# Attention and a mixture of experts in one kernel: another order of the last batch's units, of its routing products and of expert 0's evictions

## The chip, the cores and the metric

The kernel runs on one core of one Trainium2 chip. The metric is the device time of one execution in microseconds. Before the change it was 704.88 us, the median of three runs (702.8, 704.88 and 707.19).

## What is computed

Eight batches of 576 tokens pass through attention with eight heads of 64; heads 0 to 3 see a local window of 32 keys, heads 4 to 7 the keys at the same place modulo 32. Its output (4608 rows of 512) goes through a mixture of 16 experts in 4 groups:

```python
scores = np.where(masks[None], scale * q @ k.transpose(0, 1, 3, 2), -1e9)
attn   = softmax(scores) @ v                      # (8, 8, 576, 64), then x = rows of 512
g_idx  = argmax(x @ w_group)                      # one of 4 groups
e_idx  = argmax(xg @ w_expert[g])                 # one of 4 experts in it
ye     = relu(xg @ w1[g, e]) @ w2[g, e]           # 512 -> 1024 -> 512
out[token] = g_w * e_w * ye                       # weights: the two softmax values
```

## The kernel before

**Attention.** A batch is ten units. Unit j = 2u is strided unit u (heads 4 to 7), unit j = 2u + 1 is local unit u (heads 0 to 3). A unit has four parts: the score products (L206 strided, L244 local), the softmax on VectorE and ScalarE (L183 to L188; L253 to L259), the transposes of the probabilities (L212, L265) with ScalarE's copy of them out of PSUM (L215, L268), and the products with v (L222, L276) with VectorE's scaling into `xs` or `xl` (L194, L195). `attention_step` issues the scores of unit s, the transposes of unit s-4 and, at odd s, the products with v of units s-7 and s-6. In the text S0 to S4 are the strided and L0 to L4 the local units of the last batch, in the order S0 L0 S1 L1 S2 L2 S3 L3 S4 L4.

**Routing.** `logits_steps` transposes a batch's output (`loc` L328, `strd` L347) and copies it out of PSUM (L319, in the last batch L316); each of its pieces is called by `after(j)` some steps after the output of unit j. Seven batches make their logits with split float products (L361, L363). The last makes them with 24 float products of 20 columns (`rows`, L381), four for each of six tiles of 96 tokens: two of the chunks `early` (the strided heads) and two of `late` (the local heads). Then `choose` (VectorE, L415 to L423), `ranks` (TensorE, L432 to L437), `slots` and `onehots` (L459 to L487) and `table` (L491, L869) turn logits into the slots of every expert. The last batch's chain depends on itself alone, but for two sums over the batches: `k.run`, and the table of batch 6.

**Experts.** `slot_tokens` (L501) gives the indices, GpSimd gathers expert 0's rows in three blocks of 128 (L587), TensorE transposes them (L599, four for each block, one into each of PSUM banks 0 to 3), ScalarE and VectorE evict them as a high and a low half (L606, L607), and the products of the 16 experts follow (L626, L679). The first half of expert 0's first weights is loaded and split while the last batch runs (`first_half`: L569 loads, L576 ScalarE, L577 VectorE and GpSimd).

**Dummy products.** `k.spin` issues products of 512 columns (L844) that nobody reads, in places where TensorE would stand still.

**What sets the order.** Each engine works off its own queue in order. In the attention TensorE's order is the order of the code; from the last loop on, and on the other engines throughout, a planner sets it from the dependences and its own costs. The semaphores that it sets guard a PSUM bank as a whole.

Of the kernel before, what the change touches and what calls it, by code (L numbers as in the profile page):

```python
# [9 lines left out]
F32 = mybir.dt.float32  # L10
# [295 lines left out]
def logits_steps(tc, k, b, xs, xl, v):  # L306
# [16 lines left out]
    def loc(u0):  # L323
        pt = k.ps_t.next()
        w = 128 if u0 < 4 else 64
        for j, u in enumerate((u0, u0 + 1) if u0 < 4 else (4,)):
            for c in range(2):
                i = nc.tensor.transpose(pt[:, c * 256 + j * 128:c * 256 + j * 128 + w],  # L328
                                    xl[0:w, u * 256 + c * 128:u * 256 + (c + 1) * 128],
                                    k.ident[0:w, 0:w])  # L330
        if u0 == 4:
            k.spin(b, 1, i, 5)
        n = 256 if u0 < 4 else 64
        evac(lambda x: x[:, 0:2, u0 * 128:u0 * 128 + n],
             pt.rearrange("p (c x) -> p c x", c=2)[:, :, 0:n],
             lambda t: t[:, :2 * n].rearrange("p (c x) -> p c x", c=2))
# [50 lines left out]
    if last:  # L387
        lg = k.bank[1][0:TB, 0:NTB * 20].rearrange("p (t e) -> p t e", e=20)
        k.split_x, k.row = [], None
        steps = [(0, lambda: rows(range(NTB - 1), late)), (1, lambda: rows(range(NTB), early)),  # L390
                 (2, lambda: (rows(range(NTB - 1, NTB), late), k.spin(b, 2, k.row)))]
    else:
        steps = [(4, lambda: mm(0, early + late)), (5, lambda: mm(1, early + late)), (7, back)]
    return lg, {3: lambda: loc(0), 7: lambda: loc(2), 9: lambda: loc(4), 2: lambda: strd(0),
                6: lambda: strd(2), 8: lambda: strd(4)}, steps


def routing_steps(tc, k, b, lg, v, xd):
# [28 lines left out]
    def ranks():  # L427
        wide = lambda x, m: x.broadcast_to([TB, m, 16])
        with ExitStack() as order:
            if b == B - 2:  # L430
                order.enter_context(tc.issue_after(k.row.ins))
            nc.tensor.matmul(pr, k.tri, o16.rearrange("p t e -> p (t e)"), start=True, stop=True)  # L432
# [7 lines left out]
        k.spin(b, 10, i)  # L440
# [22 lines left out]
    t = (3, 5) if b == B - 1 else (7, 11) if b == B - 2 else (7, 10)  # L463
# [67 lines left out]
class Moe:  # L531
# [62 lines left out]
    def xpose(self, xs, first=False):  # L594

        nc, k = self.nc, self.k
        for blk in range(NB):
            for c in range(4):
                self.tp = nc.tensor.transpose(  # L599
                    self.bank(c)[:, blk * 128:(blk + 1) * 128].bitcast(F32R),  # L600
                    xs[blk][:, c * 128:(c + 1) * 128].bitcast(F32R), k.identr)
            if first:
                k.spin(B - 1, 6 if blk == NB - 1 else 3, self.tp, 6)
        for c in range(4):
            pt = self.bank(c)
            last = (nc.scalar.copy(self.xH[:, c, :], pt[:, :CAP]),  # L606
                    nc.vector.tensor_tensor(self.xL[:, c, :], pt[:, :CAP],  # L607
                                            self.xH[:, c, :].bitcast(F32), op=ALU.subtract))
        return last
# [190 lines left out]
def build_all(nc, d, out):  # L800
    k = Ctx()
    with tile.TileContext(nc, schedule_with_timeline_sim=True) as tc, ExitStack() as top:
# [33 lines left out]
        k.pTs = Ring([lp.tile([128, 512], F32, name=f"pTs{i}") for i in range(2)])  # L836
        tasks, now = [], [0]
# [16 lines left out]
        def batch(b, xs, xl):  # L854
# [12 lines left out]
            def table():  # L867
                k.spin(b, 16, st["add"]())
                nc.vector.tensor_tensor(k.tab, k.tab, k.misc[:, 0:2 * NSL], op=ALU.add)  # L869

            def after(j):
                store_x(tc, k, b, xd, xs, xl, j)
                if j in parts:
                    tasks.append((now[0] + (2 + j % 2 if b < B - 1 else 0), parts[j]))
# [12 lines left out]
        with ExitStack() as ms:  # L887
# [18 lines left out]
            for t in k.pT.t + k.pTs.t:  # L906
                nc.gpsimd.memset(t, 1.0)
# [24 lines left out]
            for b in range(B):  # L932
# [51 lines left out]
                for j, u in enumerate(us):  # L984
# [5 lines left out]
            k.ps_t = Ring([k.ps_t.next(), k.ps_t.next()] + k.bank[0:3])  # L990
# [58 lines left out]
```

## Time and profile before

| | us |
|---|---|
| median of 3 runs | 704.88 |
| the profiled execution | 706.36 |
| its span, first to last instruction | 704.6 |
| start to the first score product of the last batch | 173.9 |
| from there to the end of the last product with v | 38.4 (to 212.3) |
| to the end of the last batch's logits | 5.9 (to 218.2) |
| to the first product of expert 0 | 18.6 (to 236.8) |
| the 16 experts to the end of the span | 467.8 |

Times in a trace count from the span's start. A row of the timeline gives start, duration, engine, line, operation, output and input, and the number of instructions merged in it; in brackets stands the idle time ahead of it and what ended that. "PEclk" is the granted clock of TensorE, 1.00 for 2.4 GHz and 0.50 for 1.2 GHz. DVE is VectorE, ACT ScalarE, POOL GpSimd, PE TensorE, PEld its weight loads, SP the queue that issues most DMAs.

### The profile page before, as it was taken

The numbers are of one execution on the slowest core, as the hardware profiler recorded it, in microseconds if no ns is written. First come the engines' busy times: TensorE is split into PE (matmuls) and PEld (weight loads), VectorE is DVE, ScalarE is ACT, GpSimd is POOL, SyncE is SP. The second block draws the span as 40 slices with busy tenths as digits, with TensorE's granted clock in tenths as the row PEclk, the third lists the DMA queues.
The fourth block names the chain that finished last, engine by engine and source line by source line (L and its number), as shares of the span: only waits on it lengthen the run. The fifth ranks groups of instructions, "written<-read, shape, count | busy, mean of one in ns | idle before, by whom it ended". The sixth has DMA issues, their size and how long they took to land. (4 is left out here: it accounts for less than half of the span.)

```text
span 704.6 us, 15310 instructions
## 1 busy us (share of the span) xinstructions
PE 665.9 (95%) x5652; PEld 581.0 (82%) x5653; DVE 440.7 (63%) x1037; ACT 374.8 (53%) x725; POOL 259.3 (37%) x300
## 2 busy tenths in 40 slices
PE   4889999999889999999999999999999999999995
PEld 4778877877776789898898998998988989989893
DVE  8667788778856474566457656767644666545420
ACT  3666667666761473565456445656444564444421
POOL 7054556456642443134233332343240432411111
PEclk9999999999997999999999999999999999999998
DMA  9999899996341775457555474576473564744001
GB/s 274 244 270 251 214 265 246 239 236 172 123 118 33 220 256 184 151 164 252 178 187 193 171 237 136 210 271 198 152 263 124 196 220 135 260 133 149 18 18 38
DMA packets 58232, 130.34 MB, mean 185 GB/s; under 512 B 11672, under 2 KB 22168, under 8 KB 57440
## 3 DMA queue, kind: packets, MB, share of 16 engines
q1 hardware_dynamic: 50432, 109.72, 52.4%
q0 software_dynamic: 7680, 18.91, 7.5%
q8 instruction: 89, 1.46, 0.9%
q14 instruction: 31, 0.25, 0.1%
HBM read 112.86 MB, written 22.04 MB: 191 GB/s over the span
## 5 line engine op out<-in xcount | busy, mean ns | idle before, releaser
L555 DVE TENSOR_TENSOR wL<-raw,wH 128x1024 fp32r<-128x1024 f32 x122 | 145.8, 1235 | 80.9 <-ACT wH L554 75.1
L554 ACT CAST wH<-raw 128x1024 fp32r<-128x1024 f32 x124 | 124.5, 1068 | 74.8 <-PE bank L679 30.1
L626 PE MATMUL bank<-xH,wH 128*128 128x304 f32 (+10 forms) x512 | 152.9, 299 | 0.0
L626 PE MATMUL bank<-xL,wH 128*128 128x304 f32 (+10 forms) x512 | 152.7, 298 | 0.0
L626 PE MATMUL bank<-xH,wL 128*128 128x304 f32 (+10 forms) x512 | 152.7, 298 | 0.0
L663 POOL DMA_INDIRECT out<-y,idx x48 | 51.1, 1065 | 192.0 <-ACT y L657 172.9
L679 PE MATMUL bank<-wH,hH 128*128 128x512 f32 x288 | 113.3, 401 | 1.0 <-DVE hL L645 0.6
L679 PE MATMUL bank<-wL,hH 128*128 128x512 f32 x288 | 114.2, 396 | 0.0
L644 ACT ACTIVATE hH<-bank 128x384 fp32r<-128x384 f32 x128 | 62.9, 497 | 91.9 <-PE bank L626 86.2
L679 PE MATMUL bank<-wH,hL 128*128 128x512 f32 x288 | 111.0, 396 | 0.1
L645 DVE SCALAR_TENSOR_TENSOR hL<-bank,hH 128x384 fp32r<-128x384 f32 x128 | 68.8, 554 | 66.2 <-ACT hH L644 65.6
L626 PEld LDWEIGHTS bank<-xH,wH 128*128 128x128 f32 x512 | 96.5, 188 | 0.8
L626 PEld LDWEIGHTS bank<-xL,wH 128*128 128x128 f32 x512 | 96.5, 189 | 0.7
L626 PEld LDWEIGHTS bank<-xH,wL 128*128 128x128 f32 x512 | 96.5, 188 | 0.0
L587 POOL DMA_INDIRECT xg<-xd,idx x48 | 70.7, 1473 | 19.7 <-issue 10.7
L679 PEld LDWEIGHTS bank<-wH,hH 128*128 128x128 f32 x288 | 54.1, 188 | 14.6 <-issue 1.7
L679 PEld LDWEIGHTS bank<-wH,hL 128*128 128x128 f32 x288 | 54.3, 188 | 13.9 <-issue 0.6
L679 PEld LDWEIGHTS bank<-wL,hH 128*128 128x128 f32 x288 | 54.3, 188 | 12.2
L320 POOL CAST xH_r<-xf 128x512 fp32r<-128x512 f32 (+4 forms) x42 | 30.5, 726 | 75.5 <-ACT xf L319 75.5
L657 ACT ACTIVATE y<-bank,xg 128x512 f32<-128x512 f32 x48 | 31.3, 686 | 41.4 <-PE bank L679 41.4
L649 POOL CAST hP<-hH 128x512 fp32r<-128x512 f32 x16 | 9.8, 613 | 108.7 <-issue 99.1
L206 PE MATMUL bank<-sqk 128*108 128x108 f32 (+1 forms) x320 | 42.7, 279 | 6.9 <-DMA sqk<-sq 3.7
(135 smaller groups left out, 1058.3 us busy)
## 6 DMA issues: line engine op xcount, KB each, us to landing
raw<-w SPq DMA_DIRECT2D x124, 512.0 KB
vl<-vl SPq DMA_DIRECT2D x7, 877.5 KB
vs<-vs SPq DMA_DIRECT2D x7, 650.0 KB
sqk<-sqk SPq DMA_DIRECT2D x14, 324.0 KB
kl<-kl SPq DMA_DIRECT2D x7, 608.0 KB
xd<-xl SPq DMA_DIRECT2D x16, 256.0 KB
ql<-ql SPq DMA_DIRECT2D x7, 576.0 KB
sqk<-sqk SPq DMA_DIRECT2D x14, 252.0 KB
```

What stands on the lines that cost most here:

```text
L206: nc.tensor.matmul(ps[0:n, h * n:(h + 1) * n], t[:, 0:n], t[:, 2 * n:3 * n], start=True, stop=True)
L320: v.tensor_copy(sl(xH), t)
L554: nc.scalar.copy(H[:, d], r)
L555: low[j % len(low)].tensor_tensor(L[:, d], r, H[:, d].bitcast(F32), op=ALU.subtract)
L587: self.nc.gpsimd.indirect_dma_start(out=xg, out_offset=None, in_=self.xd, in_offset=bass.IndirectOffsetOnAxis(ap=self.k.idx[:, c:c + 1], a ...
L626: self.nc.tensor.matmul(ps[:, :N], a[:, c, cols], x[:, c, :N], start=(n == 0), stop=(n == last))
L644: nc.scalar.activation(self.hH[:, f, :], ps, AF.Relu)
L645: nc.vector.scalar_tensor_tensor(self.hL[:, f, :], ps, 0.0, self.hH[:, f, :].bitcast(F32), ALU.max, ALU.subtract)
L649: nc.gpsimd.tensor_copy(self.hP[:, :, i * 64:i * 64 + 64], h[:, :, s].bitcast(F32))
L657: nc.scalar.activation(y, ps, AF.Copy, scale=w)
L663: i = self.sc = nc.gpsimd.indirect_dma_start(out=self.out, out_offset=bass.IndirectOffsetOnAxis(ap=k.idx[:, c:c + 1], axis=0), in_=y, in_o ...
L679: i = nc.tensor.matmul(ps, a[:, f, s], w[:, f, :], start=(n == 0), stop=(n == 23))
```

## The change

The last batch runs its units in the order S0 S1 L0 S2 L1 S3 L2 S4 L3 L4, with two more buffers for transposed probabilities (`pE`). Its transposes go in other pieces, and its logits in four pieces, of tiles 0 to 1, 2 to 3, 0 to 3 and 4 to 5. Around the routing there are 4 dummy products behind the logits for 2, 6 behind the ranks for 10, 14 behind the table for 16, and the one with the last transposes is gone; the 12 between expert 0's transposes stay. Expert 0's three blocks are evicted in two parts, the first two blocks after the second's transposes, and the third after its own. The ranks of batch 6 no longer stand behind the last row of logits.

```diff
-    def loc(u0):
+    def loc(*us):
         pt = k.ps_t.next()
-        w = 128 if u0 < 4 else 64
-        for j, u in enumerate((u0, u0 + 1) if u0 < 4 else (4,)):
+        u0, n = us[0], 0
+        for u in us:
+            w = 128 if u < 4 else 64
...
-        if u0 == 4:
-            k.spin(b, 1, i, 5)
...
-        steps = [(0, lambda: rows(range(NTB - 1), late)), (1, lambda: rows(range(NTB), early)),
-                 (2, lambda: (rows(range(NTB - 1, NTB), late), k.spin(b, 2, k.row)))]
+        steps = [(0, lambda: rows((2, 3), late)), (0, lambda: rows((4, 5), early)),
+                 (0, lambda: (rows((4, 5), late), k.spin(b, 4, k.row)))]
+        return lg, {1: [], 3: [lambda: loc(0, 1)], 2: [lambda: strd(0)], 6: [lambda: strd(2)],
+                    5: [lambda: rows((0, 1), late), lambda: loc(2)], 8: [lambda: strd(4)],
+                    9: [lambda: rows(range(4), early), lambda: loc(3, 4)]}, steps
...
-        with ExitStack() as order:
-            if b == B - 2:
-                order.enter_context(tc.issue_after(k.row.ins))
-            nc.tensor.matmul(pr, k.tri, o16.rearrange("p t e -> p (t e)"), start=True, stop=True)
+        nc.tensor.matmul(pr, k.tri, o16.rearrange("p t e -> p (t e)"), start=True, stop=True)
...
-        k.spin(b, 10, i)
+        k.spin(b, 6, i)
...
-    t = (3, 5) if b == B - 1 else (7, 11) if b == B - 2 else (7, 10)
+    t = (3, 5) if b == B - 1 else (7, 9) if b == B - 2 else (7, 10)
...
-        for c in range(4):
-            pt = self.bank(c)
-            last = (nc.scalar.copy(self.xH[:, c, :], pt[:, :CAP]),
-                    nc.vector.tensor_tensor(self.xL[:, c, :], pt[:, :CAP],
-                                            self.xH[:, c, :].bitcast(F32), op=ALU.subtract))
+            if blk == NB - 1 or first and blk == NB - 2:
+                x = slice(blk * 128 if first and blk == NB - 1 else 0, (blk + 1) * 128)
+                for c in range(4):
+                    pt = self.bank(c)
+                    last = (nc.scalar.copy(self.xH[:, c, x], pt[:, x]),
+                            nc.vector.tensor_tensor(self.xL[:, c, x], pt[:, x],
+                                                    self.xH[:, c, x].bitcast(F32), op=ALU.subtract))
...
-                k.spin(b, 16, st["add"]())
+                k.spin(b, 14, st["add"]())
...
-                if j in parts:
-                    tasks.append((now[0] + (2 + j % 2 if b < B - 1 else 0), parts[j]))
+                for f in parts.get(j, ()):
+                    tasks.append((now[0] + (2 + j % 2 if b < B - 1 else 4 * (j == 2)), f))
...
-                for j, u in enumerate(us):
+                if b == B - 1:
+                    p, q, r = k.pTs.next(), k.pTs.next(), k.pE[0]
+                    k.pTs = Ring([p, q, p, r, q, p, r])
+                    k.pT = Ring([k.pT.next() for _ in range(6)] + k.pE[1:])
+                for j in range(10) if b < B - 1 else (0, 2, 1, 4, 3, 6, 5, 8, 7, 9):
+                    u = us[j]
...
-            k.ps_t = Ring([k.ps_t.next(), k.ps_t.next()] + k.bank[0:3])
+            k.ps_t = Ring([k.ps_t.next(), k.ps_t.next(), k.bank[0], k.bank[2]])
```

The order of the built programs shows where this reaches the other engines' queues. Lines of the changed kernel stand up to eight higher or lower than in the kernel before; PSUM bank n is `bank_(67+n)`.

**Place 1.** ScalarE at the first two pieces of expert 0's weights (`raw`, then `raw_1`), before the change: the copy of batch 6's transposes into `xf` stands between the two casts.

```order
L576 CAST wH_2853<-raw 128x512
L319 COPY xf<-bank_70 128x432
L576 CAST wH_2853<-raw_1_2864 128x512
L484 ACTIVATE rhs_t<-ohh,sm_c 96x6x48
L215 COPY pTs_125<-bank_71 126x504
```

And now:

```order
L575 CAST wH_2857<-raw 128x512
L575 CAST wH_2857<-raw_1_2868 128x512
L319 COPY xf<-bank_70 128x432
L483 ACTIVATE rhs_t<-ohh,sm_c 96x6x48
L268 COPY pT_124<-bank_71 96x512
```

The cast of `raw_1` has moved ahead of the copy out of `bank_70`. On TensorE the next transposes into `bank_70` (four of `xl`) stand behind the scores of L2 and the transposes of L0.

**Place 2.** ScalarE at the copy of batch 6's third strided piece (128x216), before the change:

```order
L259 ACTIVATE pr_120<-pr_120,mx 128x96 x2
L188 ACTIVATE pr_119<-pr_119 108x432
L259 ACTIVATE pr_120<-pr_120,mx 128x96 x2
L215 COPY pTs_126<-bank_71 108x432
L576 CAST wH_2853<-raw 128x512
L319 COPY xf<-bank_70 128x216
```

And now:

```order
L259 ACTIVATE pr_119<-pr_119,mx 128x96
L188 ACTIVATE pr_120<-pr_120 108x432
L268 COPY pT_123<-bank_71 96x512
L575 CAST wH_2857<-raw 128x512
L259 ACTIVATE pr_121<-pr_121,mx 128x96 x4
L319 COPY xf<-bank_70 128x216
```

Both times four exponentials of L3 (L259; `pr_120` before, `pr_121` now) stand ahead of the copy, but now L3's scores come after S4's, and on VectorE L3's maxima stand behind the outputs of S0 and S1 and the split of `raw_3`. TensorE has, ahead of the transposes that wait for this copy, also the four of `strd(0)` of the last batch, which need the output of S1.

**Place 3.** VectorE behind the last batch's logits (`bank_68`), before the change: the addition of batch 6's table (`tab`), for which VectorE waits for TensorE, stands third.

```order
L415 TENSOR_REDUCE mx<-bank_68 96x30
L417 TENSOR_TENSOR dl<-bank_68,mx 96x120
L869 TENSOR_TENSOR tab<-tab,bank_74 128x96
L418 SCALAR_TENSOR_TENSOR val<-dl,sm_c 96x120
L447 TENSOR_REDUCE sm<-ex 96x30
L421 TENSOR_REDUCE vm<-val 96x30
L422 TENSOR_TENSOR oh<-val,vm 96x120
L423 TENSOR_TENSOR o_3444<-oh 96x96
```

And now:

```order
L417 TENSOR_REDUCE mx<-bank_68 96x30
L419 TENSOR_TENSOR dl<-bank_68,mx 96x120
L420 SCALAR_TENSOR_TENSOR val<-dl,sm_c 96x120
L423 TENSOR_REDUCE vm<-val 96x30
L871 TENSOR_TENSOR tab<-tab,bank_74 128x96
L446 TENSOR_REDUCE sm<-ex 96x30
L424 TENSOR_TENSOR oh<-val,vm 96x120
L425 TENSOR_TENSOR o_3476<-oh 96x96
```

The addition has moved two steps back in the chain, behind `val` and `vm`. On TensorE the products that it waits for stand behind the logits in both, with 2 dummies between before and 4 now. At expert 0 the four transposes of the third block now each wait for VectorE as well as (the first) for the gather; before, they waited for the gather alone. On TensorE 20 of the 24 products of the logits stand behind the last product with v, before (6 and 14) as now (9, 4 and 7).

## Rows read from the trace of the kernel before

**Rows 1.** Busy time by stretch: TensorE, weight loads, VectorE, ScalarE, GpSimd; granted clock; DMA.
```profile
187.00:197.00 10.00, 6.55 (x101) 5.77 (x100) 9.88 (x33) 8.24 (x21) 8.62 (x12) 1.00 0.77 220
197.00:212.30 15.30, 14.89 (x194) 11.82 (x194) 7.94 (x28) 8.57 (x20) 5.04 (x7) 0.89 0.34 107
212.30:218.20 5.90, 5.83 (x57) 5.55 (x56) 3.55 (x13) 1.48 (x4) 2.59 (x6) 0.80 0.32 84
218.20:226.20 8.00, 6.49 (x32) 3.15 (x31) 4.89 (x18) 0.84 (x2) 0.94 (x4) 0.51 0.04 0
226.20:236.80 10.60, 8.89 (x45) 4.27 (x43) 3.71 (x15) 1.76 (x5) 7.50 (x7) 0.84 0.44 118
236.80:704.00 467.20, 457.82 (x2710) 410.51 (x2708) 266.88 (x344) 233.16 (x360) 139.51 (x123) 1.00 0.52 175
```

**Rows 2.** Timeline of TensorE in the last batch's attention.
```profile
189.75 0.60 PE L328 MATMUL bank<-ident,xl 128*128 128x128 f32 x4
190.28 0.56 PE L244 MATMUL bank<-kl,ql 64*64 64x96 f32 x16
192.12 0.64 PE L265 MATMUL bank<-ident,pr 128*96 128x128 f32 x4 [1.28 <-ACT pTs L215]
...
197.04 0.33 PE L328 MATMUL bank<-ident,xl 64*128 64x64 f32 x2 [1.42 <-ACT xf L319]
```

**Rows 3.** Timeline of ScalarE in the same stretch.
```profile
190.55 0.62 ACT L576 CAST wH<-raw 128x512 fp32r<-128x512 f32 x1 [1.22 <-DMA raw<-w]
...
191.51 0.56 ACT L215 COPY pTs<-bank 126x504 f32<-126x504 f32 x1
...
196.65 0.34 ACT L319 COPY xf<-bank 128x216 f32<-128x216 f32 x1
```

**Rows 4.** Waits of the queue that issues DMAs, 170 to 200 us.
```profile
SPq L569 <- PE bank L276: 2.1, 1, 2.1
```

**Rows 5.** Timeline of VectorE: two splits of expert 0's weights.
```profile
192.31 0.67 DVE L577 TENSOR_TENSOR wL<-raw,wH 128x512 fp32r<-128x512 f32 x1
...
194.29 1.71 DVE L577 TENSOR_TENSOR wL<-raw,wH 128x512 fp32r<-128x512 f32 x1
```

**Rows 6.** Timeline of TensorE from the last logits to the table.
```profile
212.51 1.20 PE L381 MATMUL bank<-cst,xH_r 128*96 128x20 f32 x12
...
214.69 3.51 PE L381 MATMUL bank<-cst,xH_r 128*96 128x20 f32 x28
...
218.85 0.69 PE L491 MATMUL bank<-rhs_t,ohl 96*128 96x96 bf16 x6
221.05 0.24 PE L432 MATMUL bank<-o,tri 96*96 96x96 bf16 x1 [1.51 <-DVE o L423]
...
221.63 4.43 PE L844 MATMUL bank<-iota 128*128 128x512 bf16 x10
...
225.93 0.48 PE L491 MATMUL bank<-rhs_t,ohl 96*128 96x96 bf16 x6
```

**Rows 7.** Timeline of VectorE in that stretch.
```profile
219.57 0.26 DVE L869 TENSOR_TENSOR tab<-tab,bank 128x96 f32<-128x96 f32 x1 [0.74 <-PE bank L491]
...
223.83 0.45 DVE L482 TENSOR_TENSOR rhs_t<-ohh,blk 96x288 bf16<-96x288 bf16 x1
```

**Rows 8.** Timeline of TensorE at expert 0.
```profile
231.23 0.54 PE L599 MATMUL bank<-identr,xg 128*128 128x128 f32 x4 [1.37 <-DMA xg<-xd,idx]
...
232.78 0.69 PE L599 MATMUL bank<-identr,xg 128*128 128x128 f32 x4 [0.35 <-DMA xg<-xd,idx]
...
234.26 0.99 PE L599 MATMUL bank<-identr,xg 128*128 128x128 f32 x4
235.05 2.11 PE L844 MATMUL bank<-iota 128*128 128x512 bf16 x6
236.81 0.49 PE L626 MATMUL bank<-xH,wH 128*128 128x296 f32 x1
```

**Rows 9.** Timeline of VectorE at expert 0.
```profile
235.56 1.95 DVE L607 TENSOR_TENSOR xL<-bank,xH 128x384 fp32r<-128x384 f32 x4 [6.53 <-ACT xH L606]
```

More of the change, by code (lines that the diff above doesn't have):

```diff
@@ L321, in evac @@
         v.tensor_tensor(sl(xL), t, sl(xH).bitcast(F32), op=ALU.subtract)
-    def loc(u0):
+    def loc(*us):
         pt = k.ps_t.next()
-        w = 128 if u0 < 4 else 64
-        for j, u in enumerate((u0, u0 + 1) if u0 < 4 else (4,)):
+        u0, n = us[0], 0
+        for u in us:
+            w = 128 if u < 4 else 64
             for c in range(2):
-                i = nc.tensor.transpose(pt[:, c * 256 + j * 128:c * 256 + j * 128 + w],
+                nc.tensor.transpose(pt[:, c * 256 + n:c * 256 + n + w],
                                     xl[0:w, u * 256 + c * 128:u * 256 + (c + 1) * 128],
                                     k.ident[0:w, 0:w])
-        if u0 == 4:
-            k.spin(b, 1, i, 5)
-        n = 256 if u0 < 4 else 64
+            n += w
         evac(lambda x: x[:, 0:2, u0 * 128:u0 * 128 + n],
@@ L389, in logits_steps @@
         k.split_x, k.row = [], None
-        steps = [(0, lambda: rows(range(NTB - 1), late)), (1, lambda: rows(range(NTB), early)),
-                 (2, lambda: (rows(range(NTB - 1, NTB), late), k.spin(b, 2, k.row)))]
+        steps = [(0, lambda: rows((2, 3), late)), (0, lambda: rows((4, 5), early)),
[3 more added lines that the diff above has]
+                    9: [lambda: rows(range(4), early), lambda: loc(3, 4)]}, steps
     else:
         steps = [(4, lambda: mm(0, early + late)), (5, lambda: mm(1, early + late)), (7, back)]
-    return lg, {3: lambda: loc(0), 7: lambda: loc(2), 9: lambda: loc(4), 2: lambda: strd(0),
-                6: lambda: strd(2), 8: lambda: strd(4)}, steps
+    return lg, {3: [lambda: loc(0, 1)], 7: [lambda: loc(2, 3)], 9: [lambda: loc(4)],
+                2: [lambda: strd(0)], 6: [lambda: strd(2)], 8: [lambda: strd(4)]}, steps
 def routing_steps(tc, k, b, lg, v, xd):
@@ L836, in build_all @@
         k.pTs = Ring([lp.tile([128, 512], F32, name=f"pTs{i}") for i in range(2)])
+        k.pE = [lp.tile([128, w], F32, name=f"pE{w}") for w in (512, 256)]
         tasks, now = [], [0]
@@ L905, in build_all @@
             clear(0)
-            for t in k.pT.t + k.pTs.t:
+            for t in k.pT.t + k.pTs.t + k.pE:
                 nc.gpsimd.memset(t, 1.0)
```

## Prediction, made before the changed kernel was run

> **What bounds the kernel now.** I read the busy times by stretch first. From 236.8 us on TensorE works 457.82 of 467.20 us at full clock [rows 1]; the change alters nothing there but the eviction of expert 0, so whatever it brings is made before 236.8. In the 63 us from the first scores of the last batch to there, TensorE is the bound where it works, and a chain through VectorE where it waits. Next the timeline of TensorE with its brackets. Between 187 and 197 us it works 6.55 of 10.00 us, 3.45 us idle [rows 1]; the two longest pieces are 1.28 us ahead of L265 and 1.42 us ahead of L328, both ended by ScalarE freeing a PSUM bank [rows 2]. ScalarE itself stands for 1.22 us at the cast of `raw_1`, waiting for a DMA [rows 3], whose queue waited 2.1 us for batch 6's last product [rows 4]: that load can't come sooner. From 197 to 212.3 TensorE is busy 14.89 of 15.30 us at a mean clock of 0.89 [rows 1]. After that comes a chain: logits to 218.2, choice, ranks, slots, table, gather, transposes, eviction, first product at 236.81 [rows 6 to 8]. The clock there is 0.80, then 0.51, then 0.84 [rows 1].
>
> The sum is made against the profiled execution, 706.36 us, which is 1.48 above the median of the runs, 704.88.
>
> **A. The order of the units and the pieces of the transposes.** TensorE's work is the same; what can change is what it waits for. Place 1: the cast of `raw_1` now stands ahead of the copy L319. It starts when the load lands, 190.55, and takes 0.53 to the next start; the copy takes some 0.5 (L215, a copy like it, 0.56) [rows 3]. So the bank comes free at about 191.65 and the transposes of `xl` start there, 0.47 earlier than L265 did at 192.12; but before, TensorE had by then done those transposes (0.53 to the next start) and one set of local scores more (0.56) [rows 2], 1.09 in all. Net 0.6 later. Place 2: before, the copy of the 128x216 piece at 196.65 released TensorE at 197.04 [rows 2, 3]. Walked by hand through the queues of the change with the durations of these rows: VectorE gets the output of S0 from TensorE at 194.4, the split of `raw_3` comes between the outputs of S0 and S1, and where it takes 1.71 [rows 5] S1 is out at 197.7 and TensorE, there since 196.1, can start `strd(0)`. L3's maxima then end about 198.3, its four exponentials about 199.0, the copy 199.3, TensorE goes on at 199.35. That is 2.3 behind 197.04, less the 0.5 of `strd(0)`, which before came later: 1.8 behind in all, the 0.6 of place 1 in it. The split took 0.67 in one case and 1.71 in the other [rows 5]. With the shorter one, 1.0 less. I take **+1.1**, between 0.8 and 1.8 and nearer to the shorter split. Bounds: -3.45, when every idle piece of that stretch goes [rows 1], and +3.5, twice the walk's 1.8, since each step of it leans on the one ahead.
>
> **B. Logits of early rows inside the attention.** By the built order the move hardly happens: 4 of 24 products stand ahead of the last product with v, before and after, and 20 behind. Eight records of 20 columns for four products cost the same in either place. What goes is one dummy, 0.22 at full clock (half of 4.43 us by 10 at the lower clock) [rows 6]: **-0.2**. If the clock held in this stretch, the 28 records would take 0.1 each, as 12 in 1.20, for 0.125, 28 in 3.51 [rows 6]: 0.7 more. Bounds -0.9 and 0.
>
> **C. Two dummies more behind the logits.** They stand ahead of batch 6's table products, for which VectorE waits in the middle of the choice (place 3). Before, it waited 0.74 there [rows 7], and the ranks came at 221.05, 2.85 behind the logits [rows 6]. Now: four dummies of 0.443 and the table products 0.69 [rows 6] end 2.46 behind the logits; the addition (0.17 to the next start), and the last three steps of the choice, some 0.7, put the ranks at 3.3. **+0.4** at the lower clock, at which this stretch ran (0.51) [rows 1]. At full clock four dummies and the products take half, 1.25, the addition has little to wait for, and the ranks come at about 2.1: -0.75, the other bound.
>
> **D. Six dummies for ten behind the ranks.** Ten ran from 221.63 for 4.43 us and held back the table products until 225.93 [rows 6], although VectorE had finished their last operand at 223.83 + 0.45 = 224.28 [rows 7]. Six end at 221.63 + 6 x 0.443 = 224.29; with the product of L510 ahead of them the table starts at 224.37. **-1.55**. It can't be more, since the operand then is the limit, and it is no less unless the operand comes later. This is the firmest term.
>
> **E. Fourteen for sixteen.** They cover part of the wait for the gather, in which TensorE stands for another 1.37 us [rows 8]. Without cover the wait is longer by their time and its end is the same: **0**.
>
> **F. Expert 0's evictions.** The second block's transposes start at 232.78 and take 0.69; VectorE's four evictions of 384 columns took 0.49 each [rows 8, 9], so those of 256 some 0.36. The first part runs, ScalarE a step ahead, from 233.5 to 235.0, one bank after the other, and the third block's fourth transpose, which waits for it, starts about 235.0, where it started before (234.26 with four in 0.99) [rows 8]. Then come the same six dummies, until 236.8 [rows 8]; VectorE's first eviction (235.56 + 0.49) was ready ahead of them already. So what the second part saves, half a microsecond, lies beside the dummies: **+0.1**. Bounds +0.6, when the first part starts late, and -0.75, when the six run at full clock (1.3 for 2.11). The Trainium skill, page "PSUM — Partial Sum Buffer", section "PSUM bank collisions raise a hardware error", speaks against this part: two engines must not be in one bank and partition quadrant at once, whatever the columns, and a kernel guards by bank. By that rule the third block's transposes can't overlap the eviction of the same banks, and the term is +0.1; if columns could be guarded apart, they would start with their data and it would be 0. No row here shows a collision.
>
> The new buffers are filled by GpSimd at the start, ahead of buffers not needed before the gather: 0.
>
> **Sum**: +1.1 - 0.2 + 0.4 - 1.55 + 0 + 0.1 = -0.15 on 706.36, or 704.7 for the median. I forecast **704.6 us**: what the routing gains, the attention loses. Chance 0.45; its own range is 702.6 to 706.2.
>
> **Rivals.**
> - *The interleaving does its work.* The strided half is out two units sooner, and with two buffers more the bank waits go; A becomes -3.45 and the sum -4.7: 700.2. For it: the waits are on copies that could come sooner. Against: the load behind the first is no earlier, and two copies stand behind more work than before (places 1 and 2). Chance 0.22.
> - *Slower: the copy behind L3's exponentials.* The mechanism of place 2 at its dear end: VectorE's split of `raw_3` is held up, S1's output, L3's maxima, the exponentials and the copy follow one by one, and the pieces of batch 6's logits, which wait for this copy by way of GpSimd, are late too. A is +3.5, the sum +2.25: 707.1. It decides when the transposes that began at 197.04 begin after 200. For it: the 1.71 us split [rows 5] and ScalarE's full queue. Against: GpSimd may be through sooner. Chance 0.20.
> - *The clock.* It was at 0.84 from 226.2 to 236.8 [rows 1], that is low for 2 x 0.16 x 10.6 = 3.4 us, and the first product came just behind. With six dummies fewer the low time may come later and fall on expert 0's products, which then lose half of it, 1.7: 706.3. The Trainium skill, "TensorE: Matmul & The Clock Gate", part 1, has the lower clock as the default that activity releases; by that rule fewer dummies can only keep it low longer. The low 0.51 of 218.2 to 226.2, ten dummies in it [rows 1, 6], agrees that dummies alone did not lift it at once. Chance 0.08.
> - Other outcomes, such as C and F at their fast ends with the clock up throughout (about 702.8): 0.05.
>
> **Numbers.** A measurement of this kernel tells about 1% from no change, 7 us; no case reaches that without a further surprise. Faster by over 1% 0.04, within 1% 0.93, slower 0.03. The range takes in nearly all of the forecast, most of the slower rival and of the clock, and reaches to just above the first rival's value: 700.6 to 707.6.
>
> **What would show it.** D: the table products start within 0.2 us of their last operand. A: TensorE's idle pieces between 187 and 200, before 3.45, and the time of the last product with v, before 212.3, forecast 213.4. C: the time from the last logit to the ranks, 3.3 for 2.85. F: the third block's transposes wait for VectorE, and the first product still follows the dummies. The forecast is wrong if the last product with v comes before 211, or if the ranks follow the logits by 2.2 or less.

## The result and the profile after

The changed kernel takes **709.19 us** (median of 16 runs, 703.32 to 713.8) beside 706.32 us before (16 runs, 699.02 to 711.82): ratio **1.0052, interval 1.0029 to 1.0074**, some 3.7 us slower. The ratio compares runs of the same rounds and leaves out those over 1.5% above the fastest of their kernel, so it is not that of the two medians (1.0041). In a second series it was 707.45 for 704.87, ratio 1.0030 (1.0002 to 1.0059). The forecast was 704.6, 0.3 us faster than before, with a range up to 707.6.

The profiled execution took 707.1 us, its span is 705.4. The busy times by stretch, with the columns and cuts of [rows 1]:

```profile
187.00:197.00 10.00, 6.94 (x90) 5.92 (x89) 6.32 (x26) 5.91 (x15) 8.45 (x12) 0.83 0.75 211
197.00:212.30 15.30, 12.60 (x186) 10.03 (x185) 8.68 (x35) 11.19 (x26) 4.54 (x7) 1.00 0.38 112
212.30:218.20 5.90, 5.90 (x77) 5.31 (x76) 4.11 (x16) 1.51 (x4) 2.53 (x6) 1.00 0.32 85
218.20:226.20 8.00, 5.64 (x47) 3.32 (x48) 6.26 (x26) 1.14 (x3) 0.90 (x4) 1.00 0.05 2
226.20:236.80 10.60, 7.01 (x29) 3.36 (x27) 3.37 (x13) 2.47 (x9) 8.18 (x8) 0.70 0.52 134
236.80:704.00 467.20, 458.51 (x2713) 410.79 (x2711) 265.78 (x342) 232.90 (x360) 137.42 (x123) 0.99 0.52 175
```

The second row has the idle time that is new: between 197 and 212.3 TensorE stands for 2.70 us where it stood for 0.41. The low clock, 3.4 us before and after, has moved from this row to the first. From 236.8 on TensorE's busy time is the same within 0.7 us. TensorE's timeline at places 1 and 2, which answers [rows 2]:

```profile
188.98 0.64 PE L265 MATMUL bank<-ident,pr 128*96 128x128 f32 x4
192.04 0.66 PE L329 MATMUL bank<-ident,xl 128*128 128x128 f32 x4 [2.41 <-ACT xf L319]
...
198.82 0.54 PE L346 MATMUL bank<-ident,xs 126*128 126x126 f32 x3 [0.58 <-DVE xs L195]
200.67 0.33 PE L329 MATMUL bank<-ident,xl 64*128 64x64 f32 x2 [1.30 <-ACT xf L319]
```

And ScalarE's, which answers [rows 3]:

```profile
190.95 0.62 ACT L575 CAST wH<-raw 128x512 fp32r<-128x512 f32 x1 [3.17 <-DMA raw<-w]
191.47 0.51 ACT L319 COPY xf<-bank 128x432 f32<-128x432 f32 x1
...
199.22 1.17 ACT L259 ACTIVATE pr<-pr,mx 128x96 f32<-128x96 f32 x4
200.29 0.32 ACT L319 COPY xf<-bank 128x216 f32<-128x216 f32 x1
```

ScalarE stands 3.17 us for the load of `raw_1`, TensorE 2.41 us for the copy behind that cast, and at place 2 the copy comes behind L3's four exponentials: the transposes that began at 197.04 begin at 200.67. The last product with v ends at 214.42 for 212.44, though the first scores of the batch stood at 173.26 for 173.91. From the one to the other it is 41.16 us for 38.54, 2.6 more. TensorE behind the attention, for [rows 6, 8]:

```profile
217.49 1.49 PE L380 MATMUL bank<-cst,xH_r 128*96 128x20 f32 x14
...
221.11 0.20 PE L431 MATMUL bank<-o,tri 96*96 96x96 bf16 x1 [1.01 <-DVE o L425]
...
221.45 1.46 PE L846 MATMUL bank<-iota 128*128 128x512 bf16 x6
...
224.27 0.43 PE L490 MATMUL bank<-rhs_t,ohl 96*128 96x96 bf16 x6 [1.35 <-DVE rhs_t L481]
...
230.26 0.70 PE L598 MATMUL bank<-identr,xg 128*128 128x128 f32 x4 [2.54 <-DMA xg<-xd,idx]
...
233.32 0.75 PE L598 MATMUL bank<-identr,xg 128*128 128x128 f32 x4 [1.05 <-DMA xg<-xd,idx]
...
234.81 1.28 PE L598 MATMUL bank<-identr,xg 128*128 128x128 f32 x4
235.90 2.12 PE L846 MATMUL bank<-iota 128*128 128x512 bf16 x6
237.67 0.49 PE L627 MATMUL bank<-xH,wH 128*128 128x296 f32 x1
```

Here the clock was full from the logits down to the gather, and the table came 1.66 us sooner than before. Then TensorE stood 2.54 us for the rows, the clock fell, and the first product is 0.86 later than before.

The time of this profile, 707.1, lies below the median of 709.19. A second profile, of the changed kernel once more, has a span of 708.5 and shows what other executions lose. Its attention by stretch (TensorE busy, granted clock, DMA share, GB/s; the batch's first scores at 174.85, its last product with v ends at 219.51):

```profile
187.00:192.00 5.00, 3.06 (x57) 1.00 0.70 168
192.00:202.00 10.00, 7.73 (x80) 0.66 0.64 214
202.00:212.00 10.00, 8.12 (x72) 0.66 0.26 85
```

TensorE waits at the same two places, 2.81 and 2.11 us, but the clock is low in both stretches of 10 us, for 2 x 0.34 x 10 = 6.8 us each. The attention is 44.7 us long instead of 41.2, with about the same idle time (6.1 and 6.3 us).

All profiles side by side, worked out from the start of the last batch's first score product (S), the end of its last product with v, and expert 0's first product. "Idle" is TensorE's, "low" the time at granted clock 0.50, all in us. The indented rows under "before" keep the old order of units, those under "change" have the new one. One execution each:

```
kernel                          S to v  (idle, low)    v to first product (low)    both
before                          38.5    (3.9,  3.4)    24.4  (13.7)                62.9
  dummies alone                 38.2    (4.9,  0.0)    20.7  ( 6.8)                58.9
  dummies alone, 20 at table    38.4    (3.7,  3.4)    22.2  (10.2)                60.6
  change in the old order       38.2    (4.9,  0.0)    22.2  (10.2)                60.4
change                          41.2    (6.3,  3.4)    23.3  ( 6.8)                64.4
change again                    44.7    (6.1, 13.7)    22.1  (10.2)                66.7
  order alone                   41.9    (6.3,  6.8)    22.1  ( 6.8)                64.0
  one eviction                  41.4    (5.3,  6.8)    21.5  (10.2)                62.9
  dummies back                  41.8    (5.5,  6.8)    22.6  ( 6.8)                64.3
  24 dummies at table           41.7    (5.9,  6.8)    22.8  (10.2)                64.4
  splits 2 to 7 later           39.6    (5.1,  3.4)    21.7  ( 5.6)                61.4
  split 1 later                 39.8    (3.9,  6.8)    21.7  (10.2)                61.5
  splits as loads land          40.3    (5.9,  3.4)    22.7  (10.2)                62.9
  the same, joined              39.8    (6.7,  0.0)    20.4  ( 6.8)                60.2
  all splits later              37.0    (2.8,  0.0)    23.7  (13.7)                60.6
  the same, joined              37.8    (2.5,  3.4)    22.3  (10.2)                60.1
  the same, joined, 20 at table 37.0    (2.8,  0.0)    20.5  ( 6.8)                57.5
```

A single profile's whole span says less than these columns: S itself lies between 170.5 and 176.1 us in the seventeen, with 0 to 6.8 us of low clock ahead of it, where the change alters next to nothing.

### The profile page after: what moved, and what is told of

It reads as the page before. It is cut to its first block, busy times and chain, and to the rows that moved or that the text cites. A ratio compares the mean times of both kernels' runs of the same rounds, so it can differ in the third digit from the quotient of the medians.

```text
span 705.4 us, 15311 instructions
## 1 busy us (share of the span) xinstructions
PE 662.2 (94%) x5647; PEld 579.5 (82%) x5648; DVE 437.5 (62%) x1041; ACT 375.9 (53%) x729; POOL 258.1 (37%) x302
## 3 DMA queue, kind: packets, MB, share of 16 engines
q8 instruction: 89, 1.46, 0.9%
## 5 line engine op out<-in xcount | busy, mean ns | idle before, releaser
L320 POOL CAST xH_r<-xf 128x512 fp32r<-128x512 f32 (+4 forms) x42 | 29.6, 706 | 75.6 <-ACT xf L319 75.6
```

The lines of the kernel that those rows point to most:

```text
L320: v.tensor_copy(sl(xH), t)
```

## The experiments

Ratios are to the kernel before, run on the same chip in the same rounds (12 runs of each experiment).

**One part alone.** The dummies, on the kernel before:

```diff
-        k.spin(b, 10, i)
+        k.spin(b, 6, i)
-                k.spin(b, 16, st["add"]())
+                k.spin(b, 14, st["add"]())
```

> The kernel before with only the dummy products changed: 6 behind the ranks and 14 behind the table, in place of 10 and 16 (D and E alone). By the sum of the prediction: table products 1.55 us earlier, the gather's first DMA and the time follow, 704.8 for a before of 706.3. By the theory that the gather waits for the stored weights (cw) and not for the indices: the first gather issue starts no earlier than 4.2 us after the store of cw is issued, so 0.8 to 1.2 us earlier than before and not 1.55, and TensorE idles longer. By the theory of the clock: TensorE, idle longer ahead of the gathered rows, runs its transposes and the dummies behind them at the low clock, the low stretch there gets longer than the 3.2 us of before (over 5), and the time is the same or up to 2 us more, 706 to 708.

702.21 us, **0.9954** (0.9926 to 0.9983). The table starts at 220.50, its operand is done at 220.44; ranks to table 3.29 us for 4.88. The gather follows the indices by 0.30 us and is issued 4.0 us behind the store of the weights, so the theory of that store does not hold here. The low clock does not last longer either: 2.5 us of it lie between the table and the first product, for 3.6 before.

The order alone, which is the changed kernel with before's eviction and these numbers:

```diff
-        k.spin(b, 6, i)
+        k.spin(b, 10, i)
-                 (0, lambda: (rows((4, 5), late), k.spin(b, 4, k.row)))]
+                 (0, lambda: (rows((4, 5), late), k.spin(b, 2, k.row)))]
-                k.spin(b, 14, st["add"]())
+                k.spin(b, 16, st["add"]())
```

> The changed kernel with the dummies (2, 10, 16) and the single eviction of before: the order of units and pieces, with the logits of early rows, alone (A and B). By the theory that the attention is what costs: the last product with v ends 2 to 2.7 us later than before reckoned from the first scores of the last batch, and the time is before +1.0 to +2.5 (the logits behind it run 1.3 us shorter). By the theory that dummies and clock make the loss: within 1 us of before. Either way ScalarE's copies at the two places of the prediction stand 2.4 and 1.3 us ahead of TensorE's transposes.

706.94 us, **1.0054** (1.0023 to 1.0086): as slow as the whole change, with the attention 3.4 us longer, more than either theory had. The order (A and B) alone is enough for the loss.

All but the order: the kernel before with the change's eviction in two parts and its dummies:

```diff
-                 (2, lambda: (rows(range(NTB - 1, NTB), late), k.spin(b, 2, k.row)))]
+                 (2, lambda: (rows(range(NTB - 1, NTB), late), k.spin(b, 4, k.row)))]
-        k.spin(b, 10, i)
+        k.spin(b, 6, i)
-                k.spin(b, 16, st["add"]())
+                k.spin(b, 14, st["add"]())
```

> The kernel before with the change's dummies (4, 6, 14) and its eviction in two parts, but with the old order of units and pieces and the logits of early rows behind the attention (A and B undone). By the theory that A costs 3 us, C 0 to 1 us, F 0.5 us and D gives 1.6: the last product with v 38.2 to 38.6 us behind the first scores, and the time 0 to 1 us less than before, about 3 less than the change. By the theory that the dummies and the clock make the loss: slower than before by 1 us or more.

705.01 us, 0.9982 (0.9951 to 1.0013), attention 38.2: what the theory of the attention had, and not slower by 1 us.

**One part undone.** The eviction:

```diff
-            if blk == NB - 1 or first and blk == NB - 2:
-                x = slice(blk * 128 if first and blk == NB - 1 else 0, (blk + 1) * 128)
...
+        for c in range(4):
+            pt = self.bank(c)
+            last = (nc.scalar.copy(self.xH[:, c, :], pt[:, :CAP]),
```

> The changed kernel with expert 0's eviction in one part as before (F undone). By the prediction: 0.1 us less than the change at most. By the theory that the first part, on VectorE, holds up the third block's transposes and so the first product: the first product starts 0.3 to 0.6 us earlier behind the landing of the third block's rows, and the time is 0.3 to 0.6 less than the change, which is too little for these rounds but not for the trace: the third block's transposes then start with their rows, with no wait for VectorE.

706.63 us, 1.0038 (1.0014 to 1.0062): the time can't tell it from the change. The trace can. TensorE at the last two blocks with one eviction:

```profile
233.85 0.54 PE L598 MATMUL bank<-identr,xg 128*128 128x128 f32 x4 [0.37 <-DMA xg<-xd,idx]
234.23 0.82 PE L844 MATMUL bank<-iota 128*128 128x512 bf16 x3
235.22 0.54 PE L598 MATMUL bank<-identr,xg 128*128 128x128 f32 x4 [0.16 <-DMA xg<-xd,idx]
235.60 1.47 PE L844 MATMUL bank<-iota 128*128 128x512 bf16 x6
237.04 0.37 PE L625 MATMUL bank<-xH,wH 128*128 128x296 f32 x1
```

And with two parts, in the run with the dummies put back, below (full clock in both):

```profile
236.43 0.53 PE L598 MATMUL bank<-identr,xg 128*128 128x128 f32 x4 [0.56 <-DMA xg<-xd,idx]
236.81 0.82 PE L846 MATMUL bank<-iota 128*128 128x512 bf16 x3
238.05 0.98 PE L598 MATMUL bank<-identr,xg 128*128 128x128 f32 x4 [0.42 <-DVE xL L608]
238.87 1.47 PE L846 MATMUL bank<-iota 128*128 128x512 bf16 x6
240.15 0.37 PE L627 MATMUL bank<-xH,wH 128*128 128x296 f32 x1
```

The third block waits for VectorE's first part and takes 0.98 for 0.54. From the second block to the first product it is 3.72 for 3.19. At full clock in that stretch, four profiles with two parts have 3.56 to 3.72 and seven with one part 3.09 to 3.27.

The dummies:

```diff
-        k.spin(b, 6, i)
+        k.spin(b, 10, i)
-                k.spin(b, 14, st["add"]())
+                k.spin(b, 16, st["add"]())
```

> The changed kernel with 10 dummies behind the ranks and 16 behind the table as before (D and E undone). By the sum of the prediction: 1.55 us more than the change, about 710.7. By the theory of the weights' store: 0.75 more. By the theory of the clock: TensorE idles less ahead of the gathered rows, the clock's low stretch before the first product of expert 0 is shorter than the 6.8 us of the change, and the time is the same or up to 2 us less, 707 to 709.

705.56 us, 1.0019 (0.9987 to 1.0051): not slower than the change, as the sum has it, but if anything faster. Its trace has ranks to table at 4.25 us (mean clock 0.57) for 3.29 in the change's second profile (0.50), so the gain of D is there in the trace; its runs have a mean granted clock of 0.987, those of the change 0.979 and 0.981. This kernel is the order alone with C and F added, and its ratio lies 0.0035 below that one's, with intervals that overlap: differences of 2 us between two kernels can't be put down to one part here.

**The clock.** More dummies ahead of the gathered rows:

```diff
-                k.spin(b, 14, st["add"]())
+                k.spin(b, 24, st["add"]())
```

> The changed kernel with 24 dummies behind the table in place of 14, so that TensorE hardly stands before the gathered rows land. By the theory of the clock (after an idle 2.5 us ahead of the gather the clock falls on the transposes and on expert 0's products): the mean granted clock of the runs rises from 0.978 towards 0.985 and the time is 1 to 2.5 us less than the change. By the theory that the attention's order alone makes the loss: the same time as the change, or up to 1 us more where the dummies run at the low clock and hold up the first transposes.

704.77 us, 1.0009 (0.9982 to 1.0037), the mean granted clock 0.987. TensorE's idle time from table to first product is 0.5 us (change: 3.6 and 2.0). The expectation of the clock's theory is met in the runs, though the profile itself has no shorter low time (10.2 us).

> The changed kernel as it is, once more, beside the others on one chip: a second profile of it and its ratio to before in the same rounds. Every theory: before +2 to +4 us. By the theory of the attention's order the last product with v again ends 41 to 42 us behind the first scores; by the theory of the clock the low stretches sum to more than in the first profile (23 us), one of them on the gather's stretch or on expert 0's products.

The change itself, in the same rounds: 1.0030 (1.0002 to 1.0059); its profile is shown above.

**The queue at places 1 and 2.** All splits but the first one unit later:

```diff
-                                 ((4, 0), (5, 1), (6, 2), (7, 3), (8, 4), (9, 5), (10, 6), (11, 7)))
+                                 ((4, 0), (6, 1), (7, 2), (8, 3), (9, 4), (10, 5), (11, 6), (12, 7)))
```

> The changed kernel with the splits of raw_1 to raw_7 one unit later, so that ScalarE's copy L319 of place 1 stands ahead of the cast of raw_1 again; nothing else differs. By the theory that place 1 makes the attention's loss (a wait of 2.3 to 2.4 us for that copy, with the clock low in the 3.4 to 6.8 us behind it in all four traces of the new order): that wait falls to 1.3 us or less, no low stretch follows it, the last product with v ends 38.5 to 40 us behind the first scores of the last batch in place of 41.2 to 41.9, and the time is 1.5 to 3 us less than the change. By the theory that place 2 (S1's output and L3's exponentials ahead of the copy) makes it: the last product with v stays at 41 or more and the time within 0.7 of the change.

703.75 us, 0.9983 (0.9956 to 1.0011), against 1.0030 to 1.0052 for the change. ScalarE:

```profile
188.11 0.52 ACT L319 COPY xf<-bank 128x432 f32<-128x432 f32 x1 [0.89 <-PE bank L346]
...
190.02 0.62 ACT L575 CAST wH<-raw 128x512 fp32r<-128x512 f32 x1
...
194.09 0.32 ACT L319 COPY xf<-bank 128x216 f32<-128x216 f32 x1
194.67 0.64 ACT L259 ACTIVATE pr<-pr,mx 128x96 f32<-128x96 f32 x2 [0.26 <-DVE mx L253]
```

And TensorE:

```profile
188.91 0.60 PE L329 MATMUL bank<-ident,xl 128*128 128x128 f32 x4
...
194.19 0.87 PE L346 MATMUL bank<-ident,xs 126*128 126x126 f32 x4 [0.75 <-DVE xs L195]
194.99 0.33 PE L329 MATMUL bank<-ident,xl 64*128 64x64 f32 x2
```

Both copies stand ahead now, `raw_1` has landed when it is cast, TensorE waits at neither place. The attention is 37.0 us long: 1.2 to 1.5 less than in the old order. So the new order of units does not lose by itself; it loses with the splits queued where the change has them.

`raw_1` alone, and then all the others alone:

```diff
-                                 ((4, 0), (5, 1), (6, 2), (7, 3), (8, 4), (9, 5), (10, 6), (11, 7)))
+                                 ((4, 0), (6, 1), (6, 2), (7, 3), (8, 4), (9, 5), (10, 6), (11, 7)))
```

> The changed kernel with the split of raw_1 alone one unit later (beside that of raw_2), the others where the change has them. ScalarE then has the copies of both places ahead, as in the run with all splits later. By the theory that this one cast, which waits 3.2 to 3.6 us for its load ahead of the copy of place 1, makes the attention's loss: the last product with v 37 to 38.5 us behind the first scores and the time 2 to 4 us less than the change, like the run with all splits later (37.0 us; 0.998 of before). By the rival that the other splits crowd ScalarE and VectorE: 40 us or more, and at most 1 us less than the change.

```diff
-                                 ((4, 0), (5, 1), (6, 2), (7, 3), (8, 4), (9, 5), (10, 6), (11, 7)))
+                                 ((4, 0), (5, 1), (7, 2), (8, 3), (9, 4), (10, 5), (11, 6), (12, 7)))
```

> The opposite: the splits of raw_2 to raw_7 one unit later, raw_1 where the change has it, ahead of the copy of place 1. By the theory of the one cast: the wait of 2.3 us or more at place 1 stays, the last product with v 41 us or more behind the first scores, and the time is within 1 us of the change, before +2 to +4. By the rival of the crowded engines: 37 to 39 us, and 2 us less than the change.

`raw_1` alone: 704.72 us, 0.9995 (0.9967 to 1.0023). Both waits for copies are gone, but VectorE's part of the split of `raw_1` now takes 2.39 us for 0.69 in the change, with GpSimd at work beside it all that time, and TensorE waits 2.61 us for S1's output, which comes behind it on VectorE. The attention is 39.8, longer than the theory's 38.5.

The others alone: 706.56 us, 1.0044 (1.0011 to 1.0078), as slow as expected, though the two medians lie only 1.2 us apart. Its profile is of its lowest time (702.8), in which `raw_1` landed 1 us sooner than in the change (the cast began 16.7 us behind S, for 17.7), the wait at place 1 was 1.45, that at place 2 2.02, and the attention took 39.6, under the 41 expected. The times lean to the theory of the one cast; the profiles say that the price hangs on the landing, and that a split moved can cost as much on VectorE.

A wait for no load, by casting what has landed:

```diff
-                                 ((4, 0), (5, 1), (6, 2), (7, 3), (8, 4), (9, 5), (10, 6), (11, 7)))
+                                 ((4, 0), (5, 2), (6, 4), (7, 1), (8, 3), (9, 5), (10, 6), (11, 7)))
```

> The changed kernel with the splits in the order in which their loads land (raw_0, 2, 4, 1, 3 in place of 0, 1, 2, 3, 4). At place 1 two casts stand ahead of the copy L319 as in the change, but the second is of raw_2, whose load landed long before; at place 2 the copy still stands behind L3's exponentials. By the theory that the wait for raw_1's load is the cause: TensorE's wait at place 1 is 1.5 us or less, the last product with v 37.5 to 39.5 us behind the first scores, and the time 2 to 3 us less than the change, 0.998 to 1.000 of before. By the rival of my forecast, the copy behind L3's exponentials (place 2): 41 us or more, and the time within 1 us of the change, 1.003 or more of before.

705.98 us, 1.0017 (0.9990 to 1.0044), attention 40.3. TensorE:

```profile
189.21 0.60 PE L329 MATMUL bank<-ident,xl 128*128 128x128 f32 x4
...
192.53 0.58 PE L212 MATMUL bank<-ident,pr 108*108 108x108 f32 x4 [1.96 <-ACT pT L268]
...
199.02 0.45 PE L329 MATMUL bank<-ident,xl 64*128 64x64 f32 x2 [2.75 <-ACT xf L319]
```

Neither theory's numbers came. The load's wait is gone, but a wait of 1.96 takes its place one copy on, since ScalarE's L483 now stands 2.55 us for VectorE. VectorE's L480, for which it stands, took 2.52 us instead of the change's 0.45: GpSimd had a split and the cast L320 beside it. Place 2 waits 2.75, behind the exponentials, so a wait there needs no late load. The test did not split the 3 us cleanly.

**Joined.** The order mended by later splits, two dummies behind the logits, one eviction; then the same with 20 dummies at the table. Beside the one eviction:

```diff
-                                 ((4, 0), (5, 1), (6, 2), (7, 3), (8, 4), (9, 5), (10, 6), (11, 7)))
+                                 ((4, 0), (6, 1), (7, 2), (8, 3), (9, 4), (10, 5), (11, 6), (12, 7)))
-                 (0, lambda: (rows((4, 5), late), k.spin(b, 4, k.row)))]
+                 (0, lambda: (rows((4, 5), late), k.spin(b, 2, k.row)))]
```

> The change with all its splits from raw_1 on one unit later, two dummies behind the logits and expert 0's eviction in one part (C and F undone, the order mended, D kept). By the terms as the runs now have them against before: attention 1.2 less, dummies behind the ranks 1.6 less, early rows 0.2 less: 3 us, 0.9955 of before or less, at least as fast as the run with the dummies alone (0.9954). By the theory that low stretches of the clock only move from place to place, the attention's gain does not show in the time: 0.997 to 1.0.

> The same as the joined kernel with 20 dummies behind the table in place of 14. By the theory of the clock, since TensorE stands less ahead of the gathered rows: a mean granted clock up to 0.003 higher and up to 1 us less than the joined kernel. By the theory that the cover only matters where TensorE stands 2.5 us there: the same time; where the 20 run at the low clock they end after the rows land, and it costs up to 1 us.

702.4 us, **0.9962** (0.9933 to 0.9990), and 703.34 us, **0.9968** (0.9939 to 0.9996). Both beat both kernels; the cover adds nothing measurable, and over the dummies alone (0.9954) the attention's 1.2 us don't show.

The joined kernel with 20 at the table, but the splits as the loads land:

```diff
-                                 ((4, 0), (6, 1), (7, 2), (8, 3), (9, 4), (10, 5), (11, 6), (12, 7)))
+                                 ((4, 0), (5, 2), (6, 4), (7, 1), (8, 3), (9, 5), (10, 6), (11, 7)))
```

> The same order of splits in the change, with two dummies behind the logits, 20 behind the table and expert 0's eviction in one part. By the terms: attention as long as in the run with the splits in landing order (0 to 1 us less than before), dummies behind the ranks 1.6 less, early rows 0.2 less: 2 to 3 us less than before, 0.996 to 0.997. If place 2 is what costs: 1.000 or more.

The dummies alone, with 20 at the table:

```diff
-                k.spin(b, 14, st["add"]())
+                k.spin(b, 20, st["add"]())
```

> The kernel before with 6 dummies behind the ranks and 20 behind the table; order, logits and eviction as before. By the terms: 1.6 us less than before, 0.9977, or 0.9954 as in the run with 6 and 14. If the mended order of the change gives anything, this kernel is 0.5 to 1.5 us slower than the joined one in the same rounds; if the attention's gain is lost to low stretches elsewhere, the two are the same.

706.44 us, 1.0033 (1.0014 to 1.0053), and 705.86 us, 1.0019 (0.9991 to 1.0046). The first differs from the joined kernel with 0.9968 in nothing but the times of the splits: the ratios differ by 0.65%, 4.6 us, and the medians by 3.1; the profiles show 2.8 in the attention. The second is the puzzle of the study: six dummies more than the kernel with 0.9954, the same attention, the same 3.29 us from ranks to table, and no gain in time. Its profile has twice the low time behind the first scores (13.7 for 6.8 us). Of the 6.7 us between the spans of the two profiles (704.5 and 697.9) only 1.7 lie from S to the first product; 2.9 lie ahead of S and 2.1 behind the first product, where the two kernels have the same code. These pairs come from different series, and two series of the change itself lay 0.2% apart, so part may be that. From ranks to table it is 3.16 to 3.35 us in every profile with six dummies, and 4.88, 4.88 and 4.25 with ten; what that is worth in time stays open.

## Why the prediction was wrong

**A is the step that failed**, as the prediction put it: "I take +1.1, between 0.8 and 1.8 and nearer to the shorter split". In five of the six profiles with the change's order of units and of splits the attention is 41.2 to 41.9 us, in the sixth 44.7, for 38.2 to 38.5 in four of the old order: **+3**, or more. The walk had the wait at place 1 too short and no price at all for the low clock around it.

The number is near the slower rival's +3.5, and that rival's mark came: the transposes of 197.04 began at 200.67, after 200. But that is mostly luck. Its mechanism was place 2 with a held-up split of `raw_3`. This split took 0.66 to 1.28 us in the six profiles, not 1.71, and TensorE waited 1.12 to 2.11 us at place 2 (mean 1.66) for 1.42 in all four of the old order, so 0.2 more. At place 1 it waited 1.85 to 2.81 (mean 2.34) for 1.23 to 1.28: 1.1 more. A third wait, for the ranks of batch 6, went from 0.79 to 1.17; the prediction did not have it. The transposes came after 200 because TensorE reached that place only at 199.37.

- Place 1. The walk let the load of `raw_1` land when it did before. It was issued at the same point (13.4 and 13.3 us behind S), but the cast that waits for it began 17.1 to 18.1 us behind S in the change's six profiles, 16.0 to 16.6 in the old order's four. Before, the copy stood ahead of that wait and lost nothing by it; now it is behind. The transposes of `xl` came at 192.04 instead of the 191.65 of the walk, with the first scores 0.65 earlier: 1.04 of error. Why the load lands later was not tried. The traces show that the two stores ahead of it on its queue are issued 0.65 us later behind S than before (10.51 and 11.31), and that between 14 and 16 us behind S the DMAs moved 0.12 to 0.31 MB in the six profiles, for 0.38 to 0.47 in the four.
- The clock. The walk priced waits at their length. In the six profiles the clock went low inside the wait at place 1 or up to 0.8 us behind its end, for 3.4 to 6.8 us. After the shorter wait there, 1.28 in [rows 2], it did so in none of four; in two of these it went low for 3.4 us some 1.6 us behind the wait at place 2. A long wait does not always bring it: the run with the splits as the loads land, joined, had waits of 1.99 and 2.75 and no low clock in the attention. What low time costs can be estimated from the two profiles of the change: about the same idle time (6.3 and 6.1), 10.2 us more of low clock, 3.5 us longer, so 0.34 us for each. Taking means of five and of four profiles, the change adds 1.5 us idle and 4.4 us low: 1.5 + 4.4 x 0.34 = 3.0 of the 3.3 between them. This is a reckoning, not a test: no run changed the clock and left the waits. The prediction had a rival for the clock, but on expert 0's products, where low clock fell in only one of the profiles for long (3.4 us, in "one eviction").
- TensorE's idle time from 187 to 200, which the prediction named as a sign, was 3.49 before and 4.29 after. The 3.45 that it gave is that of 187 to 197 [rows 1].
- The split that took 0.67 in one case and 1.71 in the other [rows 5]: in the seventeen profiles VectorE's part of a split takes 0.66 to 0.69 us where GpSimd stands still beside it, and 0.78 to 2.39 where GpSimd works throughout. So its length could not be carried over from the old order.

**B** was as forecast: last product with v to last logit 4.56 us for 4.72 at full clock in the run with the dummies alone, -0.2.

**C**: +0.4 at the lower clock was nearly right (3.12 us from logits to ranks in the second profile for the 2.85 of [rows 6], forecast 3.3), +0.3. In the first profile the clock was full and it was 2.13, which I had named as proof against me; that was the other bound. Three profiles with two dummies and the clock mostly up there (0.72 to 0.79) have 2.20 and 2.21, so at full clock the two more cost nothing.

**D** was right at the lower clock: in the second profile the table started 0.05 behind its operand (230.48 and 230.43), 3.29 us behind the ranks for 4.88 before, -1.6. In the first profile the forecast figure also came (224.27 for 225.93, 0.06 behind the operand), but by luck. There the clock was full, and TensorE stood 1.35 us for the operand with the six dummies done. Six took 1.46, so four more would have taken 0.97 and the table would have started when it did: the clock made that gain, not the missing dummies. The first gather then followed the indices by 1.26 us, for 0.31 before. The store of the weights, 4.3 us earlier, may have held it; that was argued, not tried. Twelve of the sixteen other traces have 0.30 to 0.33, among them the run with the dummies alone, whose gather came sooner behind its store.

**E**: 0 for the end of the wait, which still came with the rows (2.54 us for the DMA in the first profile). But the cover may not be free to take: in the change the kernel with 24 dummies had a mean clock of 0.987 for 0.981 in the same rounds, and 2.3 us less on the mean of its runs (705.4 for 707.7, with standard errors of 0.6 and 0.8). The Trainium skill, "TensorE: Matmul & The Clock Gate", part 1, has activity release the lower clock; these two means agree. Other runs do not fit: 20 dummies for 14 in the old order went with 0.985 for 0.988. And the two kernels with few dummies in the old order, at 0.988, show that it isn't the dummies alone.

**F** was in its range, near the upper end: +0.5 at full clock (3.72 for 3.19). At a mean clock of 0.55 to 0.60 four profiles have 4.04 to 4.35 for the 4.03 of [rows 8], so 0 to 0.3, for +0.1 forecast. VectorE's first part holds the third block, as said.

The sum with these sizes, at the lower clock: +3.0 - 0.2 + 0.3 - 1.6 + 0 + 0.3 = +1.8, to compare with 2.1 and 3.7 in the two series. The 0.3 to 1.9 us between them stay unexplained. (The prediction's own sum gave 704.7, a tenth above the 704.6 that it forecast.)

## What to carry to other kernels

Ahead of a copy that frees a PSUM bank, try to queue nothing on the same engine that waits for a DMA; a load's landing varied by 2 us from profile to profile here, and the copy takes on all of it. A new order of one engine's work must be walked through the queues of the others with the waits at their late end, and a wait of TensorE may cost more than its length, by the low clock behind it. Look also at what GpSimd does beside VectorE before carrying a duration from one order to another. When a reordering loses, look at what else was queued between its steps before undoing it: here later splits turned +3 us in the attention into -1.3.

## What the runs showed of the hardware that was not expected

A low clock was not paid at half its length in an attention with waits in it: 0.34 us for each us low in the two profiles of the change, and in the old order two profiles with 3.4 us of it were only 0.3 us longer than two with none, as TensorE idled 1.1 us less in them. Which stretch runs low changes from execution to execution of one kernel: the two profiles of the change have 3.4 and 13.7 us of it in the same work, and the times of single runs spread over 10 us. VectorE's part of one split of a 128x512 piece took 0.66 to 0.69 us with GpSimd idle beside it and up to 2.39 with GpSimd busy.
